# One loop for 31 of 32 attention tiles, with small branches for the loads that differ in its last turn

## The chip, the cores and the metric

One core of a Trainium2 chip. The time is the device time of one execution in microseconds (us), as the median of several; nearly all executions of one kernel lie within 0.1% of it here. Five engines are named: PE multiplies matrices, DVE works on vectors, ACT is the scalar engine, GpSimd has hardly anything to do in this kernel (13.1 us busy in the trace of the kernel before), and SP issues the loads. A profile traces one of these executions; its span is about 1.8 us shorter than the reported time. Times of day in the text ("at 1244 us") count from the start of a trace.

## The reference, cut to what matters

```python
def reference(A_x, A_k_cache, A_v_cache, A_wq, A_wo, B_x, B_w_gate, B_w_up, B_w_down):
    xn = _layernorm(A_x)                                     # x: 4 x 1 x 512
    q = (xn @ A_wq)                                          # 32 heads of 128
    p = softmax(q . k_cache * 128 ** -0.5)                   # k_cache: 4 x 32 x 8192 x 128, bf16
    o = p . v_cache                                          # v_cache: the same size
    return A_x + o @ A_wo + (silu(xn @ B_w_gate) * (xn @ B_w_up)) @ B_w_down
```

One token per sequence attends to a cache of 8192. K and V are 268 MB each and are read once. All the rest is small: the output weight `A_wo` (4096 x 512, 4.2 MB) is read last.

## The kernel before: the parts that matter

The 128 pairs of sequence and head are worked off in 32 tiles of 4 heads. A tile needs one K load and one V load of 8.39 MB each. Three slots of that size take turns: K of tile n lies in slot n mod 3, is turned in place and scored, and V of the same tile is then loaded over it. `finish(n)` is the softmax of tile n and the products with V of tile n-1; `begin(n+1)` turns and scores the next K.

```python
def begin(n, c, parts=(4, 4, 2, 2, 2, 2), beside=None):
    build_q(n)
    ...                          # for each part: turn K in place (DVE), then score it (PE)

def finish(n, c, load=True):
    sp = (c - 1) % NSLOT
    mx = max_1()
    pv(in_slot(sp), 0, 16)       # products of tile n-1 with its V
    rs = max_2(mx)
    pv(in_slot(sp), 16, NK)
    if load:
        load_k(n + 2, sp)        # K two tiles ahead, into the V slot just read
    row_sums(rs); pt_turn(); recip(c); fin(n - 1, c - 1)
```

All loads are issued by SP (`nc.sync`). Three tiles make one turn of the hardware loop. The last turn takes another arm, in which the tail is written out: the end of tile 30, tile 31 with its V in three parts, and the output weight in eleven loads (seven of 4 heads, four of 1 head), each consumed as it lands:

```python
with tc.For_i(0, NT + 1, NSLOT, ...) as n:
    with tc.If(n < NT - 2) as turn:
        for c in range(NSLOT):
            finish(n + c, c); begin(n + c + 1, c + 1); load_v(n + c + 1, (c + 1) % NSLOT)
    with turn.Else():
        finish(LAST - 1, LAST - 1, load=False)
        ...                                   # three loads of the last V
        begin(LAST, LAST, (2,) * 8)
        ...                                   # softmax of tile 31, products with V of tile 30
        for k in range(NB4 - 1): load_wo(k, k + 1)
        for h in range(H - HT, H): load_wo_heads(h, h + 1)
        ...
        turned()
        for k0, k1 in v_parts: pv(in_slot(2), k0, k1)
        fin(LAST, LAST, lambda: [wo_mm(i) for i in range(8)])
        for i in range(8, H): wo_mm(i)        # products with the output weight, head by head
```

Nowhere are waits written by hand: the language keeps account of who wrote which part of a buffer and puts the semaphore waits in. In the traces a load of K, V or weight adds 16 to its semaphore, one by one, and its landing is told below as the time of the last of them. In the tail eight semaphores, 114 to 121, go round.

## Time and profile before

| | before |
|---|---|
| time, median of 3 | 1280.91 us (1280.54 to 1280.94) |
| span of the trace | 1278.8 us |
| busy: DVE, PE | 62%, 55% |
| the load queue's share of the 16 DMA engines | 99.5% |
| last piece of the output weight lands | 1274.92 us |

The prediction below shows how these are read: the kernel is bound by its load stream. The timeline of the end (start, length, engine, line, operation, output from inputs, count; in brackets the idle time of the engine and what ended it):

```profile
1266.83 1.94 PE L73 MATMUL yo_ps<-slot,otn 128*4 128x256 bf16 x16
...
1271.15 0.60 PE L73 MATMUL yo_ps<-slot,otn 128*4 128x256 bf16 x8 [0.18 <-DMA slot<-in_A_wo_dram]
1272.37 0.60 PE L73 MATMUL yo_ps<-slot,otn 128*4 128x256 bf16 x8 [0.62 <-DMA slot<-in_A_wo_dram]
1273.59 0.60 PE L73 MATMUL yo_ps<-slot,otn 128*4 128x256 bf16 x8 [0.62 <-DMA slot<-in_A_wo_dram]
...
1275.74 0.30 SPq L434 DMA_DIRECT2D out_dram<-res  x1
```

Each group of products starts just after its piece of weight has landed (the waits are 0.6 us and shorter), so when the last piece is there, only its own few products are left. The store of the result is issued at 1275.74, 0.8 us after the last landing.

### The profile page before, as it was taken

The page shows a single profiled execution, that of the slowest core. Times are in us where ns is not written, and L with a number is a line of the kernel's source. Part 1 is how long each engine was busy: PE and PEld are TensorE (multiplying, and loading weights), DVE is VectorE, ACT ScalarE, POOL GpSimd, SP SyncE. Part 2 cuts the span into 40 slices and gives each one's busy share as a digit, 9 for nine tenths or more (in the row PEclk, how much of TensorE's full clock was granted, in tenths as well). Part 3 has the DMA queues.
Part 4 walks back from the last instruction along what each step waited for, and adds up shares of the span by engine and source line. Part 5 has one row for each costly group of instructions (what it writes and reads, how often), then busy time and mean ns, then how long its engine had stood idle before and what let it go on. Part 6 is the DMA issues. An engine that isn't in the chain of part 4 may idle for free.

```text
span 1278.8 us, 11722 instructions
## 1 busy us (share of the span) xinstructions
PE 698.5 (55%) x4500; PEld 307.1 (24%) x4500; DVE 790.2 (62%) x745; ACT 28.9 (2%) x70; POOL 13.1 (1%) x12
## 2 busy tenths in 40 slices
PE   1765445665445665445664445664446654446665
PEld 0322212222222222212222222221122222222222
DVE  5777655676655666655766555767556766556662
ACT  1000000000000000000000000000000000000000
POOL 3000000000000000000000000000000000000000
PEclk8877778886778777778876778877688877778877
DMA  9999999999999999999999999999999999999998
GB/s 400 452 429 428 433 434 439 426 441 426 443 428 435 433 443 428 435 433 441 430 428 439 441 430 426 441 437 435 426 441 426 445 426 439 428 443 428 433 426 337
DMA packets 11692, 550.95 MB, mean 431 GB/s; under 512 B 1304, under 2 KB 1824, under 8 KB 2720
## 3 DMA queue, kind: packets, MB, share of 16 engines
q1 hardware_dynamic: 11680, 550.78, 99.5%
q8 instruction: 9, 0.15, 0.0%
q14 instruction: 3, 0.02, 0.0%
HBM read 550.77 MB, written 0.00 MB: 431 GB/s over the span
## 4 chain that ended last, share of the span: by engine, by line
PE 44%; DVE 16%; another core or an unknown queue 14%; DMA 8%; issue 4%; DVEq 0%; ACT 0%; SPq 0%
PE sps L73 33%; DVE slot L261 9%; PE oacc L73 8%; DMA slot<-in_A_v_cache_dram 4%; DMA slot<-in_A_k_cache_dram 4%; DVE ptz L291 3%; DVE oacc L323 1%; DVE o L324 1%; PE xps L73 1%; PE mps L73 1%; DVE zq L255 1%; PE mps L277 1%; DMA slot<-in_A_wo_dram 0%; DVE rcp L300 0%
## 5 line engine op out<-in xcount | busy, mean ns | idle before, releaser
L73 PE MATMUL sps<-slot,zq 128*128 128x512 bf16 x2048 | 520.7, 418 | 387.8 <-DVE slot L261 387.8
L261 DVE STREAM_TRANSPOSE slot<-slot 128x2048 uint32<-128x2048 uint32 (+1 forms) x196 | 561.6, 2929 | 205.1 <-DMA slot<-in_A_k_cache_dram 205.1
L73 PEld LDWEIGHTS <-zq 128*128 128x128 bf16 x2048 | 211.6, 104 | 684.7 <-issue 345.7
L291 DVE STREAM_TRANSPOSE ptz<-p__117 32x512 bf16<-32x512 bf16 x128 | 90.0, 703 | 85.7 <-PE mps L73 82.7
L73 PE MATMUL oacc<-slot,ptz 128*16 128x512 bf16 x2112 | 131.7, 392 | 10.2 <-issue 5.4
L73 PE MATMUL xps<-rowy,o 128*128 128x4 f32 x66 | 18.3, 347 | 157.7 <-DVE o L324 157.7
L272 DVE TENSOR_REDUCE mx<-sps 128x1 f32<-128x512 f32 x32 | 22.1, 691 | 102.3 <-PE L73 73.0
L73 PEld LDWEIGHTS <-ptz 128*16 128x16 bf16 x2112 | 58.5, 111 | 68.7 <-issue 28.2
L73 PEld LDWEIGHTS xps<-rowy,o 128*128 128x128 f32 x66 | 16.0, 301 | 160.4 <-issue 110.5
L285 ACT ACTIVATE p__117<-sps,nb 128x512 bf16<-128x512 f32 x32 | 22.0, 688 | 1168.0 <-PE oacc L73 721.6
L255 DVE COPY zq<-qtn 32x4 bf16 (+1 forms) x128 | 29.9, 233 | 2.9
L323 DVE TENSOR_TENSOR oacc<-oacc,rowu 128x512 f32<-128x512 f32 x33 | 23.1, 699 | 11.7 <-PE yo_ps L73 10.7
L324 DVE TENSOR_REDUCE o<-oacc 128x128 f32<-128x512 f32 x33 | 22.8, 691 | 1.1
L280 DVE TENSOR_REDUCE nm<-mps 128x4 f32<-128x64 f32 x32 | 7.2, 224 | 24.8 <-PE L73 24.8
L319 DVE TENSOR_TENSOR otn_nat<-xps,rcp 128x4 f32 (+1 forms) x33 | 5.4, 163 | 23.3 <-PE xps L73 21.9
L73 PEld LDWEIGHTS mps<-rowb,rs 128*128 128x128 f32 x64 | 9.5, 187 | 13.2 <-issue 13.2
L73 PE MATMUL mps<-rowb,rs 128*128 128x4 f32 x64 | 12.3, 263 | 0.0
L277 PE MATMUL mps<-ident_f,mx 128*128 128x128 f32 x32 | 10.5, 327 | 0.0
L374 POOL MEMSET slot<- 128x11264 bf16 x1 | 9.5, 9484 | 18.9 <-DVE qtn L200 18.9
L277 PEld LDWEIGHTS mps<-ident_f,mx 128*128 128x128 f32 x32 | 4.3, 134 | 13.7 <-DVE mx L272 12.4
L73 PE MATMUL yo_ps<-slot,ident 4*4 4x256 bf16 x2 | 0.4, 368 | 13.2 <-DMA slot<-in_A_x_dram 13.2
L300 DVE RECIPROCAL rcp<-mps 128x4 f32<-128x4 f32 x32 | 5.8, 182 | 1.0
(59 smaller groups left out, 63.1 us busy)
## 6 DMA issues: line engine op xcount, KB each, us to landing
slot<-in_A_wq_dram SPq DMA_DIRECT2D x1, 4096.0 KB, 12.2
slot<-in_A_v_cache_dram SPq DMA_DIRECT2D x1, 4096.0 KB, 44.0
slot<-in_A_v_cache_dram SPq DMA_DIRECT2D x2, 2048.0 KB, 50.7
slot<-in_A_wo_dram SPq DMA_DIRECT2D x7, 512.0 KB, 21.2
slot<-in_B_w_gate_dram SPq DMA_DIRECT2D x1, 1792.0 KB, 16.6
slot<-in_B_w_up_dram SPq DMA_DIRECT2D x1, 1792.0 KB, 19.6
slot<-in_B_w_down_dram SPq DMA_DIRECT2D x1, 1792.0 KB, 22.5
slot<-in_A_k_cache_dram SPq DMA_DIRECT2D x32, 51.7
```

The lines of the kernel that those rows point to most:

```text
L73: nc.tensor.matmul(out_ap, lhsT=lhsT, rhs=rhs, start=start, stop=True, skip_group_check=True, **kw)
L255: nc.vector.tensor_copy(out=zq[q0:q1, :, XO + a * QB], in_=qtn[q0:q1, bass.ds(n * 4, 4)])
L261: nc.vector.transpose(out=ap, in_=ap)
L272: nc.vector.reduce_max(out=mx[:], in_=sps[:], axis=AX.X)
L277: nc.tensor.matmul(mps[:, 0:P], lhsT=mx[:, 0:1].to_broadcast([P, P]), rhs=ident_f[:, :], is_transpose=True, start=True, stop=True, skip_gr ...
L280: nc.vector.tensor_reduce(out=nm[:], in_=by_row(mps[:, 0:P]), axis=AX.X, op=ALU.max, negate=True)
L285: nc.scalar.activation(out=p_[:], in_=sps[:], func=ACT.Exp, bias=nb[:, 0:1], scale=qscale, accum_out=rs[:])
L291: nc.vector.transpose(out=ptz[y * QB:(y + 1) * QB, :, y, :, :].rearrange("p s u x -> p s (u x)"), in_=p_[y * QB:(y + 1) * QB, :].rearrange ...
L300: nc.vector.reciprocal(out=rcp[c % NSLOT][:], in_=mps[:, P:P + HT])
L323: nc.vector.tensor_tensor(out=o_, in0=o_, in1=rowu[:].unsqueeze(2).to_broadcast([P, NV, Dh]), op=ALU.mult)
L324: nc.vector.reduce_sum(out=o1[:], in_=o_.rearrange("p u d -> p d u"), axis=AX.X)
L374: nc.gpsimd.memset(slot[2][:, w3:SLOT], 0.0)
```

## The change

The tail's tile 30 and half of tile 31 are a copy of what the loop does, apart from which loads are issued. So the loop is made to cover them: the last turn goes through the same instructions, and small branches choose the loads. The program gets shorter: the trace has six fetches of 16 KB of instructions (0.10 MB) instead of nine (0.15 MB).

```diff
-    def finish(n, c, load=True):
+    def finish(n, c, load):
...
-        if load:
-            load_k(n + 2, sp)
+        load()
...
+    def load_last_v():                        # three loads of the last V, into slot 2
...
+    def load_all_wo():                        # eleven loads of the output weight, into slot 0
+        for k in range(NB4 - 1):
+            load_wo(k, k + 1)
+        for h in range(H - HT, H):
+            load_wo_heads(h, h + 1)
...
+        def next_k(c):
+            def load():
+                with tc.If(n < NT - 2) as more:
+                    load_k(within(n) + c + 2, (c - 1) % NSLOT)
+                with more.Else():
+                    if c == 0:
+                        load_last_v()
+                    else:
+                        load_all_wo()
+            return load
+
+        finish(n, 0, next_k(0))
+        begin(n + 1, 1)
+        with tc.If(n < NT - 2):
+            load_v(within(n) + 1, 1)
+        finish(n + 1, 1, next_k(1))
         with tc.If(n < NT - 2) as turn:
...                                            # tile n + 2 and the scores of tile n + 3
         with turn.Else():
-            finish(LAST - 1, LAST - 1, load=False)
...                                            # the copy of tiles 30 and 31, and its loads
             turned()
             for k0, k1 in v_parts:
                 pv(in_slot(2), k0, k1)
             fin(LAST, LAST, lambda: [wo_mm(i) for i in range(8)])
             for i in range(8, H):
                 wo_mm(i)
```

The weight loads are now issued in a small branch, the products with them stand in the last one.

More of the change, by code (lines that the diff above doesn't have):

```diff
@@ L378 @@
     ffn_down()
-    with tc.For_i(0, NT + 1, NSLOT, iteration_sync="reg_based", hint_engines=[]) as n:
-        with tc.If(n < NT - 2) as turn:
-            n = nc.s_assert_within(n, 0, NT - 2 - NSLOT, skip_runtime_bounds_check_because="the arm has n < NT - 2")
-            for c in range(NSLOT):
-                finish(n + c, c)
-                begin(n + c + 1, c + 1)
-                load_v(n + c + 1, (c + 1) % NSLOT)
-        with turn.Else():
-            finish(LAST - 1, LAST - 1, load=False)
-            wo_t = slot[0]
-            def load_wo(k0, k1):
-                nc.sync.dma_start(out=wo_t[:, k0 * 4 * D:k1 * 4 * D].rearrange("p (k c e) -> p k (c e)", c=4, e=D),
-                                  in_=A_wo[k0 * 4 * P:k1 * 4 * P, :].rearrange("(k p c) e -> p k (c e)", p=P, c=4))
-            def load_wo_heads(h0, h1):
-                nc.sync.dma_start(out=wo_t[:, h0 * D:h1 * D].rearrange("p (h e) -> p h e", e=D),
-                                  in_=A_wo[h0 * P:h1 * P, :].rearrange("(h p) e -> p h e", p=P))
-            def wo_mm(i):
-                lhsT = otn[:, i, :] if i < H - HT else otn_nat[:, HT:].rearrange("p (b h) -> p b h", b=B)[:, :, i]
-                yo_mm(lhsT, wo_t[:, i * D:(i + 1) * D])
-            def load_v_part(k0, k1):
-                nc.sync.dma_start(out=slot[2][:, k0 * 512:k1 * 512], in_=v_all[LAST, :, k0 * 512:k1 * 512])
-            v_parts = ((0, NK // 2), (NK // 2, 3 * NK // 4), (3 * NK // 4, NK))
-            for k0, k1 in v_parts:
-                load_v_part(k0, k1)
-            begin(LAST, LAST, (2,) * 8)
-            v30 = in_slot(0)
-            mx = max_1()
-            pv(v30, 0, 16)
-            rs = max_2(mx)
-            pv(v30, 16, NK)
-            for k in range(NB4 - 1):
-                load_wo(k, k + 1)
-            for h in range(H - HT, H):
-                load_wo_heads(h, h + 1)
-            pt_turn()
-            row_sums(rs)
-            recip(LAST)
-            fin(LAST - 1, LAST - 1)
@@ new lines, with load_wo, load_wo_heads, wo_mm @@
+    wo_t = slot[0]
+    def load_wo(k0, k1):
+        nc.sync.dma_start(out=wo_t[:, k0 * 4 * D:k1 * 4 * D].rearrange("p (k c e) -> p k (c e)", c=4, e=D),
+                          in_=A_wo[k0 * 4 * P:k1 * 4 * P, :].rearrange("(k p c) e -> p k (c e)", p=P, c=4))
+    def load_wo_heads(h0, h1):
+        nc.sync.dma_start(out=wo_t[:, h0 * D:h1 * D].rearrange("p (h e) -> p h e", e=D),
+                          in_=A_wo[h0 * P:h1 * P, :].rearrange("(h p) e -> p h e", p=P))
+    def wo_mm(i):
+        lhsT = otn[:, i, :] if i < H - HT else otn_nat[:, HT:].rearrange("p (b h) -> p b h", b=B)[:, :, i]
+        yo_mm(lhsT, wo_t[:, i * D:(i + 1) * D])
@@ new lines, with within @@
+    v_parts = ((0, NK // 2), (NK // 2, 3 * NK // 4), (3 * NK // 4, NK))
+    def load_last_v():
+        for k0, k1 in v_parts:
+            nc.sync.dma_start(out=slot[2][:, k0 * 512:k1 * 512], in_=v_all[LAST, :, k0 * 512:k1 * 512])
+    def load_all_wo():
[3 more added lines that the diff above has]
+            load_wo_heads(h, h + 1)
+    with tc.For_i(0, NT + 1, NSLOT, iteration_sync="reg_based", hint_engines=[]) as n:
+        def within(n):
+            return nc.s_assert_within(n, 0, NT - 2 - NSLOT, skip_runtime_bounds_check_because="the arm has n < NT - 2")
+        def next_k(c):
[13 more added lines that the diff above has]
+        finish(n + 1, 1, next_k(1))
+        with tc.If(n < NT - 2) as turn:
+            m = within(n)
+            begin(m + 2, 2)
+            load_v(m + 2, 2)
+            finish(m + 2, 2, lambda: load_k(m + 4, 1))
+            begin(m + 3, 0)
+            load_v(m + 3, 0)
+        with turn.Else():
```

## The prediction

> **What bounds the kernel now.** I read the page's busy table and queue table first, then a table of stretches, then the waits, the issues and the last chain.
>
> ```profile
> span 1278.8 us, 11722 instructions
> PE 698.5 (55%) x4500; PEld 307.1 (24%) x4500; DVE 790.2 (62%) x745; ACT 28.9 (2%) x70; POOL 13.1 (1%) x12
> q1 hardware_dynamic: 11680, 550.78, 99.5%
> HBM read 550.77 MB, written 0.00 MB: 431 GB/s over the span
> ```
>
> No compute engine is busy for more than 62% of the span, while the one load queue keeps the 16 DMA engines busy for 99.5% of it. The next view (stretch, its length, busy time of PE, PEld, DVE, ACT, POOL, clock, DMA share, GB/s) shows whether this is so everywhere.
>
> ```profile
> 200.00:1160.00 960.00, 520.64 (x3300) 229.05 (x3298) 593.91 (x548) 19.47 (x50) 0.00 (x0) 0.76 1.00 434
> 1245.00:1260.00 15.00, 9.47 (x129) 4.63 (x125) 6.24 (x13) 0.78 (x2) 0.00 (x0) 0.79 0.98 419
> 1265.00:1275.00 10.00, 8.32 (x82) 4.77 (x81) 1.55 (x3) 0.00 (x0) 0.00 (x0) 0.72 0.80 318
> 1275.00:1279.00 4.00, 0.24 (x2) 0.04 (x1) 0.41 (x1) 0.36 (x1) 0.00 (x0) 0.82 0.00 1
> ```
>
> In the loop the DMA share is 1.00 at 434 GB/s. A tile is 8.39 MB of K and 8.39 MB of V, so at 434 GB/s it takes 38.7 us, and K landings in the trace are 38.7 us apart (1186.33, 1225.08). The tail stays at the stream's rate until the last piece of the output weight lands at 1274.92 by the landing records; then 3.9 us of casts, store and closing remain.
>
> Compute's slack is in the waits (engine, line, releaser: total, times, longest):
>
> ```profile
> DVE slot L261 <- DMA slot<-in_A_k_cache_dram: 205.1, 30, 8.0
> ```
>
> DVE stands still 205.1/30 = 6.8 us per tile for the next K. The slack of the issuing side is in the issues, whose last number is the time from issue to landing:
>
> ```profile
> slot<-in_A_k_cache_dram SPq DMA_DIRECT2D x32, 51.7
> slot<-in_A_v_cache_dram SPq DMA_DIRECT2D x31, 37.1
> ```
>
> One load alone takes 8.39 MB / 434 GB/s = 19.3 us. A K load is therefore issued 51.7 - 19.3 = 32.4 us before the queue reaches it, a V load 37.1 - 19.3 = 17.8 us. To cost time, a branch on the issuing engine (SP) must delay a V load by more than about 17.8 us. The landing records agree: the V load issued at 1207.28 had a K load ahead of it that landed at 1225.08.
>
> The tail's issues and the end of the chain:
>
> ```profile
> 1207.28 0.33 SPq L98 DMA_DIRECT2D slot<-in_A_v_cache_dram  x1
> 1210.03 2.41 SPq L404 DMA_DIRECT2D slot<-in_A_v_cache_dram  x3
> 1245.36 13.90 SPq L392 DMA_DIRECT2D slot<-in_A_wo_dram  x7
> 1265.19 3.87 SPq L396 DMA_DIRECT2D slot<-in_A_wo_dram  x4
> ...
> ```
> ```profile
> 1210.85 48.03 DMA slot<-in_A_v_cache_dram
> ...
> 1260.70 4.42 another core or an unknown queue
> 1265.17 1.90 PE oacc L73 x15
> 1267.07 1.66 PE yo_ps L73 x15
> 1268.73 6.19 DMA slot<-in_A_wo_dram
> ```
>
> The end is set by transfers: the last V parts, then the output weight. PE, which the chain names between them, is waiting for landings.
>
> [...] The trace has 40 to 50 ns for SP's and 77 to 208 ns for PE's[...]. [...] The trace has no fetch of instructions between 173 and 1211 us, so the loop of three tiles runs without them; the 16 KB fetches of the last stretch (1211, 1248, 1263 us) took about 0.95 us each on a DMA engine. [...] the sixth output-weight load takes over the semaphore of the first V part and is issued at 1254.10, 0.06 us after that part's landing at 1254.04.
>
> **The change part by part.**
> Removed: the unrolled copy of tile 30's end, tile 31's scores and its softmax. The same instructions now run from the loop's body. Data operations and bytes are equal, so no load time is removed: 0 us.
> Loop branches: PE, DVE and ACT have one branch per turn before and after; it moves from the turn's start to the place after the second tile, just ahead of a K wait. On PE the whole turn's end plus the branch took from 1088.03 to 1089.02, 1.0 us, and this now falls into DVE's 6.8 us of waiting. 0 us.
> Small branches: three per turn, holding only loads. GpSimd, with no work in the loop, has no branch there in the trace, so I expect engines other than SP to have none for these. On SP the present branch costs about 0.2 us at entry (1092.59 to 1092.77) and 0.3 us at the arm's end (1091.68 to 1091.97). Three are about 1.5 us per turn, each about 0.5 us against 17.8 or 32.4 us of queued work: hidden, 0 us.
> Bookkeeping of the arms: when arms hold different numbers of loads, their semaphores must be brought level. The present arm does this for two semaphores with a wait and an add just before its end, at 1091.77 and 1091.85. In the new kernel one load stands against three, then one against eleven, so more semaphores must be levelled, and one can belong to a V load still in flight. That V lands at 1205.62 in the last full turn, and the next V is issued at 1207.28 because of its scores; the earlier turns have 1.3 to 2.2 us between the two. Waiting for the older V is thus nearly free, and anything over is inside the 17.8 us. 0 us.
> Last turn: tile 31 now turns K in pieces 4, 4, 2, ... instead of 2, 2, .... The first takes 4.46 us instead of half as long. From K landing to the end of the scores, the loop's form takes 1207.25 - 1186.36 = 20.9 us and the present tail's 1244.7 - 1225.17 = 19.5. So +1.4 us for the scores and for the first output-weight issue (1245.36 to about 1246.8); V31 keeps the queue full until 1265.13, 18 us later. The products with the first V parts started at 1254.98; with 1.4 us and 1.0 us of branch they start at 1257.4 and end after 3.6 + 1.8 us at 1262.8, before the last part lands at 1265.13. Hidden. What is left visible: a different order of semaphores for the weight loads, for which I allow +0.4 us.
> Sum: 1280.9 + 0.4 = 1281.3 us.
>
> **The rivals.**
> First: an arm's end waits for the K load that it has just issued. Then the next V is issued at that K's landing instead of 33.7 us after its issue (1173.62 to 1207.28), 51.5 - 33.7 = 18 us late, and the queue runs empty. By the start of the kernel (first issue 0.74, first packet 1.78 us) I estimate 1.5 to 3 us of gap. One such wait per turn for ten turns gives 15 to 30 us (about 1296 to 1311), two give up to 1341. Against it: in the present arm the levelling of a semaphore that also carries a load stands ahead of that load (1092.77, then the issue on it at 1096.04). For it: eleven loads over eight semaphores must be levelled every turn.
> Second: an instruction fetch or a late weight load at the final branch. PE has 2.3 us before the last V part lands and, as its work after that part ends at about 1271 while the last weight piece lands at 1274.92, some 3.5 us more. A stall must pass about 5 us to show. If SP is held by a V part's semaphore until 1265 with few weight loads queued, the queue gaps once: +2 to 4 us, 1283 to 1285.
> Third: a gain from the shorter program. Fetches are 0.0% of the DMA time, so at most 0.5 us.
>
> **Range and chances.** The sum says no change; the second rival gives the upper side up to 1286, and the low side is the run-to-run spread and a slightly better tail, 1279.5. The first rival is the only way past 2% (1306.5): it needs more than 25 us, 2.5 us per turn, and I give it 5%. No path leads 2% down, since the bytes at 434 GB/s alone take 550.77 / 0.434 = 1269 us: 1%. The rest, 94%, is within 2%.
>
> **What would show it.** Right: the stretch from 200 to 1160 us stays at 1.00 and 434 GB/s, DVE still waits about 6.8 us per tile for K, issue to landing stays well above 20 us, SP has three more branches per turn and other engines none, the last weight piece lands within 3 us of 1274.9. Wrong: issue-to-landing of V near 20 us with SP waiting on a load's semaphore (first rival); a hole in the DMA share after 1245 us (second); branches or instruction fetches on PE and DVE for the small branches.

## The result, and the profile after

| | before | after |
|---|---|---|
| time, median of 6 | 1280.68 us | 1285.03 us (1284.22 to 1285.31) |
| ratio | | 1.0033, 95% interval 1.0020 to 1.0046 |
| span of the trace | 1278.8 us | 1283.0 us |
| last load lands | 1274.92 us | 1273.71 us |
| from there to the end of the span | 3.9 us | 9.3 us |

Ratios are the mean time of one kernel's runs over that of the other's of the same rounds, so not quite the ratio of the medians. The changed kernel is 4.3 us slower: inside the predicted range and inside "within 2%", but about ten times the 0.4 us that the sum had allowed. The last two rows say where to look: the transfers end 1.2 us earlier, what follows them takes 5.4 us longer, and 5.4 - 1.2 is the 4.2 us of the span.

First the loop, since the prediction spent most of its words on it. Two lines of the page of the changed kernel, and its table of stretches (columns as in the prediction):

```profile
span 1283.0 us, 12347 instructions
q1 hardware_dynamic: 11680, 550.78, 99.2%
```
```profile
200.00:1160.00 960.00, 520.73 (x3300) 229.33 (x3299) 594.15 (x548) 19.47 (x50) 0.00 (x0) 0.76 1.00 434
1265.00:1275.00 10.00, 2.15 (x21) 0.96 (x16) 1.39 (x2) 0.00 (x0) 0.00 (x0) 0.50 0.76 304
1275.00:1283.00 8.00, 4.29 (x50) 2.91 (x50) 0.57 (x2) 0.36 (x1) 0.00 (x0) 0.83 0.00 1
```

From 200 to 1160 us the DMA share is 1.00 at 434 GB/s as before, and the last K lands at 1224.88 us against 1225.08. The loop has lost nothing. In the stretch from 1265 to 1275 PE was busy for 8.32 us before and is busy for 2.15 us now; its work comes after 1275, when the DMA share is 0.00.

The loop's issuing did change. SP's waits in the changed kernel (engine and line, waited for what: total, times, longest), then two neighbouring loads of the loop, before and after:

```profile
SPq L412 <- SPq L412: 484.5, 29, 19.0
```
```profile
1091.29 0.33 SPq L98 DMA_DIRECT2D slot<-in_A_v_cache_dram  x1
1096.04 0.33 SPq L95 DMA_DIRECT2D slot<-in_A_k_cache_dram  x1
1129.60 0.33 SPq L98 DMA_DIRECT2D slot<-in_A_v_cache_dram  x1
```
```profile
1091.35 0.33 SPq L98 DMA_DIRECT2D slot<-in_A_v_cache_dram  x1
1109.32 0.33 SPq L95 DMA_DIRECT2D slot<-in_A_k_cache_dram  x1
1129.63 0.33 SPq L98 DMA_DIRECT2D slot<-in_A_v_cache_dram  x1
```

L412 is the small branch around the K load. Its K load is issued 13 us later than before, because its semaphore, 114, is still taken by the K load ahead of it, which lands at 1109.0 (SP waits on 114 until 1109.01); then SP stands at the end of the arm until the V load in flight has landed, up to 19 us. And the next V load is issued at the same time as before. The K load that lost 13 us still lands 38.3 us after its issue, where a transfer alone takes 19.3 (from one landing at 1128.29 to the next at 1147.59): the queue never knew.

Now the end. The chain that ended last, and the timeline, both of the changed kernel:

```profile
1263.64 1.31 PE oacc L73 x13
1264.96 8.12 DMA slot<-in_A_wo_dram
1273.07 0.04 issue
1273.11 1.87 PE yo_ps L73 x16
1274.98 0.52 PE xps L73 x2
1275.51 4.00 PE yo_ps L73 x48
```
```profile
1273.11 1.87 PE L73 MATMUL yo_ps<-slot,otn 128*4 128x256 bf16 x16 [7.85 <-DMA slot<-in_A_wo_dram]
1274.91 0.50 PEld L73 LDWEIGHTS xps<-rowy,o 128*128 128x128 f32 x2 [0.43 <-issue]
...
1275.43 3.12 PEld L73 LDWEIGHTS <-otn 128*4 128x4 bf16 x40
...
1279.94 0.30 SPq L444 DMA_DIRECT2D out_dram<-res  x1
```

PE stands idle for 7.85 us before the first product with the output weight, though the first piece of weight had landed at 1264.89. It starts at 1273.11, 0.04 us after another landing. Which one, the landing records say (issue, semaphore, landing; worked out from the trace):

```
piece           issued   semaphore  landed
heads 0 to 3    1246.04  118        1264.89
heads 4 to 7    1246.54  119        1266.13
...
head 28         1264.18  117        1272.67
head 29         1264.96  118        1273.07    <- what the first product waited for
head 30         1266.20  119        1273.41
head 31         1267.41  120        1273.71
```

Head 29 uses the same semaphore, 118, as heads 0 to 3. So all 64 products, which before were done in the shadow of the transfers, come when nearly all transfers are over: from 1273.11 to 1279.3 us.

### The profile page after: what moved, and what is told of

Its sections match the earlier page's. It is cut to its first block, busy times and chain, and to the rows that moved or that the text cites.

```text
span 1283.0 us, 12347 instructions
## 1 busy us (share of the span) xinstructions
PE 695.9 (54%) x4500; PEld 307.1 (24%) x4500; DVE 790.4 (62%) x743; ACT 28.9 (2%) x70; POOL 13.1 (1%) x12
## 5 line engine op out<-in xcount | busy, mean ns | idle before, releaser
L261 DVE STREAM_TRANSPOSE slot<-slot 128x2048 uint32<-128x2048 uint32 (+1 forms) x194 | 561.5, 2958 | 205.1 <-SPq L412 72.1
L73 PE MATMUL yo_ps<-slot,otn 128*4 128x256 bf16 x56 | 5.3, 365 | 7.8 <-DMA slot<-in_A_wo_dram 7.8
```

Source lines behind the costliest of these rows:

```text
L73: nc.tensor.matmul(out_ap, lhsT=lhsT, rhs=rhs, start=start, stop=True, skip_group_check=True, **kw)
L261: nc.vector.transpose(out=ap, in_=ap)
```

## The experiments

The first four tell apart why the first product waits. **Theory A**: behind the end of a branch (the join), the exact count inside the arm is lost, and a reader waits for everything that the arm put on the semaphore. **Theory B**: PE is late because of the loop's form of tile 31 and the branches. **Theory C**: the loads themselves come in a worse order. A second question was why the transfers end 1.2 us earlier: because instructions are no longer fetched then (theory F), or because the last V is issued later (theory G).

**e1, weight loads out of the small branch.**

```diff
-                with more.Else():
-                    if c == 0:
+                if c == 0:
+                    with more.Else():
                         load_last_v()
-                    else:
-                        load_all_wo()
...
         with turn.Else():
+            load_all_wo()
             turned()
```

> The changed kernel with one part undone: the eleven output-weight loads leave the small branch and stand at the head of the last branch, beside the products that use them. Theory A (behind the join of the small branch, a product waits for everything that its arm put on the semaphore, so the first product waits for the first one-head load, 8 us after its own piece): the first product on the output weight starts within 0.5 us of the first weight piece's landing, near 1265 to 1266 us, the last landing stays near 1273.7, the span falls by about 5 us to some 1277.5 to 1278, the time to 1279 to 1280 us, below the kernel before. Theory B (PE is late because of the loop's form of tile 31 and its branches): time stays at 1284 to 1285. Theory C (the weight loads are issued too late or in a worse order): the last landing itself moves, and the first product still waits.

Measured: 1279.60 us (1279.37 to 1279.76, 5 runs; before 1280.61). Timeline:

```profile
1265.18 2.16 PE L73 MATMUL yo_ps<-slot,otn 128*4 128x256 bf16 x16 [0.32 <-DMA slot<-in_A_wo_dram]
```

The first product starts 0.14 us after its piece (1265.04), the last load lands at 1273.86. B and C fall: tile 31 and the loop's branches are as in the changed kernel. All of the loss is in where the weight loads stand. It also beats the kernel before by 1.0 us; the ranges of single runs don't overlap (before: 1280.35 to 1280.99), though the interval of the ratio, 0.9979 to 1.0006, does not exclude equality.

**e2, eight loads on eight semaphores.** All in the small branch as in the changed kernel.

```diff
-        for h in range(H - HT, H):
-            load_wo_heads(h, h + 1)
+        load_wo_heads(H - HT, H)
```

> The changed kernel with all loads left in the small branch, but the four one-head loads of the output weight made one load: eight loads on eight semaphores, so none carries two pieces. Theory A in its narrow form (sharing a semaphore inside the arm is what costs): the first product starts at its own piece's landing, about 1265 us, and the time falls to 1279 to 1280.5 us (the last piece is four heads instead of one, which leaves about 0.3 us more of products after the last landing). Theory A in a wide form (behind a join everything of the arm is waited for, shared or not): the first product still waits until about 1273, time 1284 to 1285. Theory B: 1284 to 1285.

Measured: 1279.82 us (1279.77 to 1280.45). First product at 1264.95, its piece landed at 1264.91. So being loaded in a branch costs nothing by itself; a shared semaphore is needed for the loss.

**e3, the same eleven loads in another order.**

```diff
-        for k in range(NB4 - 1):
-            load_wo(k, k + 1)
         for h in range(H - HT, H):
             load_wo_heads(h, h + 1)
+        for k in range(NB4 - 1):
+            load_wo(k, k + 1)
```

> The changed kernel with the same eleven loads in the small branch in another order: the four one-head loads first, then the seven four-head loads. Theory A, narrow form: now the one-head loads share their semaphores with weight pieces 4, 5 and 6, which are used late anyway or land last; the first four-head pieces have semaphores of their own, so the first product starts at about 1265 to 1267 us and the time is 1279 to 1281 us. Wide form or theory B: 1284 to 1285 us. If the number of loads mattered rather than who shares with whom, nothing would change here.

Measured: 1283.96 us (1282.70 to 1284.23). A miss for theory A:

```profile
1271.45 1.87 PE L73 MATMUL yo_ps<-slot,otn 128*4 128x256 bf16 x16 [6.64 <-DMA slot<-in_A_wo_dram]
```

Here heads 0 to 3 have semaphore 114 to themselves inside the arm and landed at 1266.32. In the trace, PE first waits on 118, until 1271.34, and only then on 114. On 118 are head 28 (1264.04) and heads 16 to 19 (landed at 1271.32), with which the first product has nothing to do. What is special about 118 is that in the loop's turns the *other* arm of this branch issues its K load on it, into the same slot 0.

**e4, the kernel before with the eleven loads in a branch that is always taken.**

```diff
-            for k in range(NB4 - 1):
-                load_wo(k, k + 1)
-            for h in range(H - HT, H):
-                load_wo_heads(h, h + 1)
+            with tc.If(n > 0):
+                for k in range(NB4 - 1):
+                    load_wo(k, k + 1)
+                for h in range(H - HT, H):
+                    load_wo_heads(h, h + 1)
```

> The kernel before, with one thing added: the eleven output-weight loads stand in a small branch of their own, whose condition is always true there. The unrolled tail, its order and all else stay. Theory A: the cost appears without the rest of the change: the first product on the output weight waits for the second piece on its semaphore, a one-head load, and starts near 1274 us instead of 1266.8; about 6 us of products follow, and the time rises by 4.5 to 6 us to 1285 to 1287 us. Theory B (form of tile 31, branches in the loop): a branch that only SP takes costs nothing here, 1280.5 to 1281.5 us.

Measured: 1280.48 us (before: 1280.67), first product at 1266.81 as in the kernel before. Semaphores 117, 118 and 119 each carry two pieces here, and no product that needs the first waits for the second. Theory A is dead.

What fits e1 to e4 is **theory D**. Behind the join, a reader of the slot must wait for whoever may have written it: the piece of weight of one arm, and the K load of the other. For the K load it waits for the count that 118 would have after the K arm. The arms are made level, so that count is the total at the join, and in the arm that did run, 118 reaches it only with the second load on it. The product waits for a load that was not issued, and its stand-in is whatever comes last on that semaphore. In e2, 118 carries one load, so the total is the first piece itself; in e4 there is no other arm. The changed kernel, built once more from its record for this check, has just these waits written in it: its first product waits on 118 for two loads (32) above the count before the arm, its next group on 119 for one (16), and the K arm adds 16 to 118 to level it before the K load adds its own 16. The experiments that follow test the theory by its cause.

**e10, a K load that never runs.** e4 with a second arm. `n > 0` always holds there, so the added load is never issued.

```diff
-            with tc.If(n > 0):
+            with tc.If(n > 0) as always:
...
+            with always.Else():
+                load_k(0, 0)                  # slot 0, where the weight lies
```

> The kernel before with the eleven weight loads in a small branch (as in the run where that cost nothing) and, as its second arm, one K load into the slot where the weight lies, which never runs. Theory D: behind the join, a reader of the slot waits for the last load of either arm that wrote it; in the arm that ran, the semaphore of the other arm's K load reaches that count only with the second weight load on it (the second one-head piece, landing at 1274.3). So the first product starts at about 1274.3 instead of 1266.8, some 6 us of products follow, and the time rises by 4.5 to 6 us, to 1285 to 1287, by a load that is never issued. Theory A (a branch's join alone blurs the pieces) was already contradicted and would give 1280.5 here, as without the second arm.

Measured: 1286.10 us (1285.43 to 1286.66; before 1280.60), ratio 1.0045 (1.0031 to 1.0058).

```profile
1274.36 1.87 PE L73 MATMUL yo_ps<-slot,otn 128*4 128x256 bf16 x16 [7.42 <-DMA slot<-in_A_wo_dram]
```

The second piece on 117 lands at 1274.32. A load that is never issued costs 5.5 us.

**e11, the same with the never-run load going to slot 1.**

```diff
-                load_k(0, 0)
+                load_k(0, 1)
```

> The same with the never-run K load going into another slot, which no later instruction reads. Theory D (the wait comes from the slot's other writer): no cost, first product at 1266.8, time 1280.3 to 1281. Theory D2 (the wait comes from any load of the other arm, through the semaphores alone): as with the same slot, 1285 to 1287.

Measured: 1280.51 us (before 1280.60), first product:

```profile
1266.68 1.94 PE L73 MATMUL yo_ps<-slot,otn 128*4 128x256 bf16 x16
```

Same branch, same semaphores, same number of loads: only the slot of a load that doesn't run differs, and the 5.5 us are gone. D2 (the wait comes from any load of the other arm, whatever its slot) falls, D stands.

**e9, the changed kernel with the weight in another slot.** Slot 1 held the last K, which has been scored by then.

```diff
-    wo_t = slot[0]
+    wo_t = slot[1]
```

> The changed kernel with all its branches and loads, but the output weight put into the slot that held the last K instead of the one that the other arm's K load fills. Theory D: nothing in the other arm of that branch writes this slot, so the products wait for their own pieces: first product near 1265 us, time 1279 to 1280.5. If the wait came from the join and its semaphores whatever the slot: 1284 to 1285.

Measured: 1279.63 us (1279.47 to 1279.71; before 1280.60), first product at 1265.13 after its piece at 1265.00. One character undoes the loss, with every branch and every load of the change in place.

**e5, the last V's loads out of the branch too** (on top of e1).

```diff
-                if c == 0:
-                    with more.Else():
-                        load_last_v()
...
         with turn.Else():
+            load_last_v()
             load_all_wo()
```

> e1 with the three loads of the last V moved to the head of the last branch too, so no small branch has a second arm. In the changed kernel the first part was issued at 1225 and the others at 1244 us, because they waited for semaphores of loads in flight. If issue times are hidden (predicted: the queue holds 18 us and more of work), this changes nothing: time within 0.7 us of e1, last landing 1273.3 to 1274. If the late issue of the V parts cost or gained stream time, the last landing moves by over 1 us.

Measured: 1279.61 us (1279.54 to 1279.67), last landing 1273.75. The three parts were issued at 1210, 1225 and 1244 us here, in e1 at 1211 to 1212, in the changed kernel at 1225, 1244 and 1245, and the last V part landed at 1263.65, 1263.76 and 1263.60. Issue times inside the queued work made no difference (1279.61 against 1279.60 us in e1). This also speaks against G, which had the earlier end come from late V issues.

**e8, an issue late enough to matter.** The changed kernel with one K load per turn put behind the next V load.

```diff
-            finish(m + 2, 2, lambda: load_k(m + 4, 1))
+            finish(m + 2, 2, lambda: None)
             begin(m + 3, 0)
             load_v(m + 3, 0)
+            load_k(m + 4, 1)
```

> The changed kernel with one K load per turn issued some 34 us later: behind the V load of the next tile instead of ahead of it. This tests the step of the prediction that says that a late issue is free as long as it stays inside the work already queued (about 32 us for a K load). Here it doesn't: the queue should run dry once a turn, for the 1.7 us from the older V's landing to the issue[...], and V comes ahead of K, so compute waits longer. Expected: 3 to 5 us per turn, ten turns, 1315 to 1335 us, with the mean GB/s from 200 to 1160 us falling below 425. If issue times did not matter at all (transfers limited by something else), it stays at 1285 us.

Measured: 1360.34 us (2 runs), and in its table of stretches:

```profile
200.00:1160.00 960.00, 489.91 (x3192) 218.98 (x3192) 575.50 (x528) 18.69 (x48) 0.00 (x0) 0.76 0.95 409
```

The DMA share falls to 0.95. The direction was right, the size only about half of what came: (1360.3 - 1285.0) / 10 turns = 7.5 us per turn instead of 3 to 5. The landing records show two holes per turn where one was expected: 22.9 us instead of 19.3 between two landings at 802 us (V issued at 780.60, when the queue had been empty since 779.55) and again at 864 us. The second fits this: the K now lands one transfer later, so its V is issued late in its turn (at 842.14, when the queue had been empty since 841.10). So here a late issue was free up to the queued work (e5) and not beyond it.

**e6, bringing instruction fetches back.** One of the 16 increments of a load falls behind in the kernel before. In us after the first, from the landing records:

```
before, 2nd part of the last V:  seven at 0 to 0.55, nine at 1.44 to 1.80
before, 3rd part (fetch at 1263.1): seven at 0 to 0.56, eight at 1.45 to 1.80, one at 3.19
after,  3rd part:                nine at 0 to 0.46, seven at 1.43 to 1.75
```

In the kernel before the last increment stays 1.1 to 1.4 us behind the other fifteen to the end (2.87 against 1.73 us in the last load). That each increment is the work of one of the page's 16 DMA engines is the author's reading of the equal numbers; the records name no engine. The queue tables of the stretch from 1180 to 1275 us, before and then after, show one thing that differs there:

```profile
q1 hardware_dynamic: 2487, 39.26, 96.4%
q8 instruction: 3, 0.05, 0.2%
```
```profile
q1 hardware_dynamic: 2487, 39.26, 96.3%
```

The longer tail was fetched as it came up (three blocks of 16 KB, 0.93 to 0.96 us each, at 1211, 1248 and 1263 us); the shorter program has no fetch there. e6 adds 280 harmless instructions to e1, between the products with the second and the third part of the last V:

```diff
...
+            junk = psX.tile([P, HT], dt.float32, name="xps")
+            for i in range(140):
+                mm(junk[0:QB, :], ident[:, 0:QB], ident[:, 0:HT], start=True)
...
```

> e1 with 140 tiny products (280 instructions of PE) into a scratch tile, put between the products of the second and the third part of the last V, where PE waits 2.8 us anyway. This asks about the last landing, 1274.9 us before and 1273.7 in the changed kernel. Theory F (an instruction fetch during the last transfers makes one of the 16 DMA engines about 1.2 us late, and every later landing waits for it): the trace shows a 16 KB fetch of instructions in the last 50 us again, the 16th increment of each later transfer comes 1.1 to 1.4 us after the 15th, the last landing is near 1274.9 and the time about 1 us above e1. Rival G (the last landing is earlier because the V parts are issued late, one after the other): no change, last landing 1273.7, time as e1. The tiny products themselves take some 3 us of PE and should be hidden before the last V part.

Measured: 1281.70 us, last landing 1273.93: a miss for F as it was put. The fetches are there (1260 and 1268 us), but after each, one increment moved from the early group to the late one (nine early ones, then eight, then seven), and the last landing hardly moved (1273.86 in e1). The time is longer because the tiny products took 6.9 us instead of the 3 expected and made PE late. In the kernel before, the first two fetches of the tail moved an early increment likewise (nine, then eight, then seven early ones); after its third, at 1263 us, one of the late ones came at 3.19 us instead of at most 1.8.

**e7, more tiny products, at the start.** e6 with 128 further tiny products where PE waits for the first load.

> The padded kernel of the fetch test with 128 further tiny products (256 instructions of PE[...]) at the start, where PE waits for its first load. In the padded kernel the 7th fetch (1260 us) and the 8th (1268 us) each moved one engine's increments back by about 1.3 us, but engines that are 1.3 us ahead of the others, so nothing was lost; in the kernel before, the 7th and 8th did the same and the 9th (1263 us) hit a late engine. Theory F, refined (a fetch costs its engine 1.2 us, and the end only if that engine is among the late ones; which one is fixed by the fetch's number): here the fetches of the tail are numbers 8 and 9, so the 16th increment of the transfers after about 1268 us falls 1.2 us behind the 15th and the last landing moves from 1273.9 to about 1275. If the engine is not fixed by the number, or the fetch is not the cause, the last landing stays at 1273.9. (The time itself is set by PE in this kernel and may not move.)

Measured: the fetches of the tail came at 1259.3 and 1266.3 us; from the transfer landing at 1268.87 on, one increment came at 3.2 us after the first, fifteen by 1.64, and the last load landed at 1275.09 instead of 1273.93. That is F as refined, called in advance. The time (1280.89 us, 1280.51 to 1282.85) is not compared: PE is late in this kernel for its tiny products, as in e6.

| kernel | first product starts | last load lands | time, us |
|---|---|---|---|
| before | 1266.83 | 1274.92 | 1280.6 to 1280.7 |
| after | 1273.11 | 1273.71 | 1285.03 |
| e1, weight loads in the last branch | 1265.18 | 1273.86 | 1279.60 |
| e2, eight loads | 1264.95 | 1273.71 | 1279.82 |
| e3, one-head loads first | 1271.45 | 1273.79 | 1283.96 |
| e4, before + branch | 1266.81 | 1274.90 | 1280.48 |
| e5, V loads out too | 1265.05 | 1273.75 | 1279.61 |
| e9, weight in slot 1 | 1265.13 | 1273.84 | 1279.63 |
| e10, never-run K load, slot 0 | 1274.36 | 1274.95 | 1286.10 |
| e11, never-run K load, slot 1 | 1266.68 | 1274.94 | 1280.51 |

## Why the prediction was right or wrong

**Bound: right.** The stream sets the time, in the loop at 1.00 and 434 GB/s before and after.

**Removed work, loop branch: right.** No load time was gained, and no time lost in the loop (last K at 1224.88 against 1225.08).

**Small branches: cost right, a reason wrong.** "I expect engines other than SP to have none" failed: in the changed trace every engine, GpSimd too, has 96 compare-and-branches instead of 33. The inference came from a look at GpSimd from 60 us on. It has 33 in the kernel before as well; having nothing to wait for, it had run through all turns between 23 and 29 us. The cost was zero all the same: DVE's idle time before it turns K is 205.1 us in both kernels, so the branches in front of that wait took nothing from the loop.

**Bookkeeping of the arms: right in the loop, and closer to the edge than it sounds.** SP does wait for the older V at an arm's end (up to 19.0 us), and a K load loses 13 us of its lead by waiting for its semaphore. Both stay inside the queued work, as the step said, and e5 and e8 show that this is the reason: inside it nothing is lost, beyond it 7.5 us per turn. The first rival (SP held until the K load just issued has landed) did not happen. Three of the prediction's readings are a little narrow, though nothing hangs on them: from a V's landing to the next V's issue the loop has 0.8 to 2.5 us over all its turns, not 1.3 to 2.2; SP's branches take 38 to 59 ns in the trace of the kernel before, not 40 to 50, and PE's 77 to 251 ns, not 77 to 208, with one of 6.8 us (at 160.8 us, as the loop is first run through).

**Last turn: this is the step that failed**, in the term "a different order of semaphores for the weight loads, for which I allow +0.4 us". In its place the runs show +5.4 us between the last landing and the end, from products that wait for a stand-in of the K load in the other arm (e3, e9, e10, e11). The step followed what SP waits for when it issues and left out what PE waits for when it reads. The other terms of that step held: the weight issues began at 1246.04 (1246.8 predicted), the products with the first two V parts ended at 1260.9 (1262.8 predicted), before the last part.

**Second rival: right size, wrong mechanism.** It gave 1283 to 1285 us for a hole in the queue. There was none; the last load landed earlier than before. PE was late for a wait that no rival named. Its 5 us of slack before a stall shows fit e6: there 6.9 us of added PE work made the time 2.1 us longer than e1's, so about 4.8 us were hidden.

**Third rival: too small.** "At most 0.5 us" for the shorter program came from the fetches' share of DMA time. From the fetch at 1263 us on, one of each load's 16 increments came 1.1 to 1.4 us behind the other fifteen, and every later load was complete only with it: 1274.92 - 1273.71 = 1.2 us. The loss hid this gain: 5.4 - 1.2 = 4.2 us.

So the time fell inside the range because its upper side had been widened for a stall in the tail, not because the stall had been foreseen. What no run here shows is which DMA engine takes a fetch or why, nor that an increment that falls behind is that engine's; that it goes by the fetch's number is only consistent with the traces in which it was counted.

## What to carry to other kernels

When loads move into a branch and their readers stay outside, ask what the other arm writes into the same buffer: as this program was built, readers behind the join waited for both writers, and the one that did not run was represented by the last load on its semaphore (7.42 us of waiting and 1286.10 us in e10, against 1280.51 us in e11). Keep such loads beside their readers (e1), give the arms different buffers (e9), or put one load on each semaphore (e2). And read a tail twice, once for when transfers are issued and land, once for when their readers may start.
